# First block's q and k turned by the tensor engine instead of by transposing DMAs, in a kernel of attention and two MLP stages with a written-out sequence

## The chip, the cores and the metric

One core of one Trainium2 chip runs the whole program. The metric is the device time of one execution in microseconds. Before the change, three runs gave 931.09 us as their median (930.62 to 933.18).

## The reference, cut to what matters

```
attention: q, k, v are (4 batches, 8 heads, 576 positions, 64), s is (4, 8, 576)
  scores = q k^T / 8, causal, plus min(-(cum_i - cum_j), 0) with cum = cumsum(max(s, 0))
  out    = softmax(scores) v                      -> x, 2304 rows of 512
first MLP:  h = x w_in (512 to 2048);  x = (h - tanh(h)) w_out
second MLP: a = x w_a, b = x w_b (512 to 1536);  out = (a * b) w_out
```

Heads and batches of attention are independent; each row of x passes through both MLPs by itself.

## The kernel before, in words

Numbers are carried as a high and a low 16-bit part, so that a product of two 32-bit matrices becomes three matmuls of 16-bit parts. Splitting into parts is elementwise work for VectorE (DVE), ScalarE (ACT) and GpSimd (POOL), and there is much of it: q, k, v, the attention weights, x, the hidden values, and all MLP weights, which come as words of 64 bits.

Queries are taken in blocks. Block 0 is batch 0, positions 0 to 255, and its four head pairs are four *units*. For a unit, `qk_split` (L1086) makes the split tile `qk` of 8 slices of 128 columns (four of q, then four of k; in each slice the high and the low part beside each other). `u_turn` (L1107) turns these slices, so that the head dimension lies on partitions: one transposing DMA on SP's queue (`turn`, L1102) writes all 8 slices into `qkT`. Two copies then put half of the partitions (64 of 128) of `qkT` into `qB` and `kB`. These tiles hold three further partitions, the bias rows, which `u_split` (a scaled constant) and `u_load` (a DMA) fill. `u_qk` multiplies `qkT` and then `qB`/`kB` into one sum, `u_exp` and `u_norm` make the split weights `a`. In block 0 the weights are already turned by PE: `u_norm` multiplies each slice with the unit matrix `eyeh` into a `qk` bank and copies it out into `aT`. `u_pv` multiplies with v.

Block 0 goes through the first MLP with unsplit 32-bit matmuls (`l1_mm`, L1315, and `l2_mm`, L1350), because the weights are not yet split; later blocks use split weights.

Operations are recorded in program order, with the engines that may do each (`either`, L356; `copy_scaled`, L930, allows ACT, DVE, and POOL unless its source is PSUM). The string `ORDER` (L38) then fixes both the order of issue and the engine of each: `follow` (L445) reads three characters as one number, whose last two bits choose the engine and whose other bits name the operation. Each engine works through its own operations in that order; semaphores hold one back until its inputs and buffers are ready. Nearly all instructions carry the line of the helper that calls the engine, L647, so the profile is read by tile names. In those names, `qk` is the split tile, the PSUM banks of the scores and the banks of the turned tiles, `ws` and `raw` hold loaded q, k and v, `w` the MLP weights, `zs` the exponentials, `xf` the attention output. POOL instructions that read, and DVE instructions that read two SBUF tiles or copy from SBUF to SBUF fast, are marked by `shares` (L659), and a marked POOL instruction is made to wait for the marked DVE instruction ahead of it in the order.

Of the kernel before, what the change touches and what calls it, by code (L numbers as in the profile page):

```python
# [41 lines left out]
    "AFNAFgAMYAQIAGUAGgAQMAGkAKJAGoAHgAHkAG9APcAPkAYUAh0AHoAPsAGuAPgAH8AP0AGwAHAAHuAG0AZIAHEAh8AKBAHwAG5AHIAKQAKUAKYAKcAKgAH0"
    "AKkAJmAIAALQAFkAMuAM1AKoAQgALcAIEAP4AIIAYYAiQAKsAKyAM6AM8ALBAH5ALEAP8ALIAXwAK0ALgANIAJpALUALYALkANAARAANEAQwARQAlcAYcANM"
    "ANQALMAX0AX4AX8ALoAYgALsALyAK4AYAAK8AMBANUAYEAZQAL0AMEAIMANYANeAIRANtAN8AL4AL9AYIANwAOAAMIAiMAOIANhAUQAPoANkAYOAMMAiIAN0"
    "AYkAOEAjIAiUAOMAOQANpAiYAicAUYAikAigAOUAQkAN4AioAixAOYAMQAOeAOtAisAYoATwAOwAO0Ai9AOgAOkAQoAMVAlqAT4AO5AOoAO8AliAjAAQsAjV"
# [2002 lines left out]
```

## Time and profile before

| what | value |
|---|---|
| median of three runs | 931.09 us |
| the profiled execution | 930.71 us, of which the span of the core is 928.9 us |
| PE busy | 881.3 us (95% of the span), 7650 matmuls |
| DVE busy | 805.7 us (87%) |
| ACT busy | 574.1 us (62%) |
| POOL busy | 346.1 us (37%) |
| DMA queue on SP | 55.6% of 16 engines' span |

The span is counted from the first to the last instruction. Shares over the whole span hide the stages: attention of block 0, then the first MLP between the attention of the following blocks, then the second MLP. So the stretches have to be read one by one. PE is TensorE's matmul row; its ends are modelled.

### The profile page before, as it was taken

To read this page: it belongs to the slowest core of one execution; us is meant where nothing else is said; L and a number is where in the kernel's file an instruction comes from. 1 tells how busy PE (TensorE), PEld (TensorE's weight loads), DVE (VectorE), ACT (ScalarE), POOL (GpSimd) and SP (SyncE) were. 2 spreads that over 40 slices of the span, in tenths; PEclk is the share of its full clock that TensorE was granted. 3 is DMA by queue.
4 is the path that set the end of the run, shared out by engine and by line. 5 is a ranking of instruction groups with operands and counts; after the bars stand their busy time and mean duration, and the time that the engine had idled before them with its cause. 6 is when DMAs were issued, how large, how long until landed. Compare 5 with 4: busy or idle time off the path is not lost.

```text
span 928.9 us, 20616 instructions
## 1 busy us (share of the span) xinstructions
PE 881.3 (95%) x7650; PEld 647.6 (70%) x7650; DVE 805.7 (87%) x2011; ACT 574.1 (62%) x1136; POOL 346.1 (37%) x495
## 2 busy tenths in 40 slices
...
GB/s 204 304 214 238 231 123 124 113 154 171 206 165 174 193 179 167 208 137 161 308 206 189 84 24 1 69 2 1 47 54 53 60 185 65 62 72 112 72 68 115
DMA packets 260197, 123.38 MB, mean 133 GB/s; under 512 B 228544, under 2 KB 236976, under 8 KB 260096
## 3 DMA queue, kind: packets, MB, share of 16 engines
q1 hardware_dynamic: 259936, 121.79, 55.6%
q8 instruction: 60, 0.98, 0.4%
q14 instruction: 41, 0.34, 0.1%
q10 hardware_dynamic: 160, 0.26, 0.1%
...
## 4 chain that ended last, share of the span: by engine, by line
PE 47%; DVE 5%; issue 2%; DMA 1%; POOL 1%; ACT 0%; SPq 0%; POOLq 0%; DVEq 0%; ACTq 0%
PE h L647 16%; PE qk L647 12%; PE acc L647 11%; PE pv L647 8%; DVE w L647 1%; DVE x2f L647 1%; DVE g L647 1%; DMA x2f<-pb_d 0%; DMA out_dram<-x2f 0%; DVE a L647 0%; DVE ghl L647 0%; DVE sq L647 0%; DVE xf L647 0%; DVE h L647 0%; DVE th L647 0%
## 5 line engine op out<-in xcount | busy, mean ns | idle before, releaser
L647 PEld LDWEIGHTS <-w 128*128 128x128 f16 x3840 | 372.2, 98 | 67.0 <-issue 4.0
L647 PE MATMUL h<-xhl,w 128*128 128x256 f16 x2256 | 276.9, 273 | 2.4 <-DVE ghl L647 1.1
L647 PE MATMUL acc<-w,ghl 128*128 128x512 f16 (+1 forms) x1092 | 233.6, 358 | 0.9 <-DVE sq L647 0.9
L647 PEld LDWEIGHTS <-ghl 128*128 128x128 f16 x1290 | 123.6, 98 | 99.9 <-issue 4.8
L647 PE MATMUL h<-xf,w 128*128 128x256 f16 (+1 forms) x416 | 71.3, 310 | 0.0
L647 DVE CUSTOM_DVE_ANT_0 qk<-qk,caus,cs 128x384 f32<-128x384 f32 (+3 forms) x120 | 64.9, 555 | 2.8 <-PE qk L647 1.4
L647 PE MATMUL qk<-xf,w 128*128 128x256 f16 x432 | 55.2, 273 | 0.8 <-DVE xf L647 0.6
L647 PE MATMUL pv<-xf,w 128*128 128x256 f16 x432 | 55.0, 273 | 0.0
L647 ACT ACTIVATE g<-h 128x512 f32<-128x512 f32 x40 | 23.4, 592 | 48.8 <-PE h L647 27.0
L647 ACT ACTIVATE w<-w 128x1024 f32<-128x1024 f32 (+1 forms) x45 | 50.9, 1156 | 1.4 <-DVE w L647 1.4
L647 ACT ACTIVATE th<-h,xc 128x512 f32<-128x512 f32 x64 | 43.7, 683 | 9.5 <-PE h L647 7.4
L647 PE MATMUL qk<-qkT 128*128 128x128 f16 (+4 forms) x168 | 45.7, 316 | 3.7 <-ACT zs L647 3.1
L647 PE MATMUL qk<-kB,qB 67*128 67x128 f16 (+4 forms) x168 | 45.3, 313 | 3.9 <-ACT zs L647 2.2
L647 PEld LDWEIGHTS <-v 128*64 128x64 f16 x1440 | 37.7, 113 | 12.8 <-issue 10.8
L647 PEld LDWEIGHTS <-x2f 128*128 128x128 f16 x360 | 35.1, 98 | 7.1 <-DMA x2f<-pb_d 0.8
L647 DVE SCALAR_TENSOR_TENSOR h<-h,xc,th 128x512 f32<-128x512 f32 x48 | 36.0, 751 | 1.6 <-ACT th L647 1.6
L647 ACT ACTIVATE zs<-qk,nm 128x128 f32<-128x128 f32 (+1 forms) x64 | 30.2, 472 | 11.2 <-DVE nm L647 9.4
L647 DVE SCALAR_TENSOR_TENSOR ghl<-h,xsg,ghl 128x512 f16<-128x512 f32 x48 | 35.8, 746 | 1.4 <-ACT ghl L647 0.9
L647 DVE SCALAR_TENSOR_TENSOR a<-qk,sm,a 128x512 f16<-128x512 f32 (+1 forms) x56 | 35.2, 630 | 1.4 <-ACT a L647 1.0
L647 ACT ACTIVATE qk<-qk,nm 128x512 f32<-128x512 f32 (+1 forms) x56 | 31.7, 566 | 7.4 <-DVE nm L647 5.4
L647 ACT ACTIVATE sq<-qk 128x512 f32<-128x512 f32 x22 | 13.1, 594 | 37.4 <-PE qk L647 35.0
L647 PE MATMUL pv<-aT,v 128*64 128x128 f16 x960 | 34.5, 225 | 1.3 <-DVE aT L647 0.8
...
## 6 DMA issues: line engine op xcount, KB each, us to landing
...
```

The costliest lines, as they stand in the source:

```text
L647: return getattr(getattr(plan.nc, name), what)(*[real(a) for a in args], **{k: real(a) for k, a in kw.items()})
```

## The change

In `u_turn` the units of block 0 (`u.j == 0`) no longer issue the transposing DMA. Each unit instead fills two PSUM banks, one with its four q slices and one with its four k slices, by matmuls with `eyeh`; each bank is copied whole into `qkT` and, by a second copy of 64 partitions, into `qB` or `kB`. A copy that reads PSUM may go to ACT or DVE, not to POOL. All other units keep the old code.

`ORDER` is replaced as a whole. The number of recorded operations goes from 4569 to 4581 (three more in each of four units).

```diff
 ORDER = (
-    "AAMAAEAB0AAIAAQAAUAAAAAYABsAB4ABoABwAAcAAgAAkAAsAAwAA0ABEABJABNABSAAoAA4AA8ABAABVABZABkACEACAAB8ACIACMACQACYAQQAIkACUACc"
...
 )
@@
         qkT = anew(u, [P, n + u.sk, P], F16, "qkT")
-        turn(qkT, u.qk.rearrange("p a e d -> p (a e d)"))
-        copy_scaled(u.kB[0:D], qkT[0:D, n:], 1.0)
-        copy_scaled(u.qB[0:D], qkT[D:P, 0:n], 1.0)
+        if u.j == 0:
+            for which in range(2):
+                pt = bank("qk", 3)
+                pl.hold = (qkT, u.qB if which == 0 else u.kB)
+                a0, m = (0, n) if which == 0 else (n, u.sk)
+                with pl.group():
+                    for i in range(m):
+                        pl.tensor.matmul(
+                            pt[:, i * P:(i + 1) * P], u.qk[:, a0 + i].rearrange("p e d -> p (e d)"), eyeh,
+                            start=(i == 0), stop=True, skip_group_check=True)
+                pt = pt[:, 0:m * P].rearrange("p (a c) -> p a c", c=P)
+                copy_scaled(qkT[:, a0:a0 + m], pt, 1.0, True)
+                if which == 0:
+                    copy_scaled(u.qB[0:D], pt[D:P], 1.0, True)
+                else:
+                    copy_scaled(u.kB[0:D], pt[0:D], 1.0, True)
+        else:
+            turn(qkT, u.qk.rearrange("p a e d -> p (a e d)"))
+            copy_scaled(u.kB[0:D], qkT[0:D, n:], 1.0)
+            copy_scaled(u.qB[0:D], qkT[D:P, 0:n], 1.0)
```

## Rows read from the trace of the kernel before

**Rows 1.** Busy time by stretch: PE, PEld, DVE, ACT, POOL (instructions), granted clock, DMA share, GB/s
```profile
9.40:39.60 30.20, 14.69 (x109) 9.20 (x110) 29.38 (x115) 28.56 (x72) 12.54 (x24) 1.00 1.00 243
39.60:113.00 73.40, 66.88 (x355) 42.52 (x355) 71.13 (x218) 69.96 (x134) 22.93 (x40) 0.98 0.94 241
113.00:440.00 327.00, 324.27 (x3302) 217.39 (x3300) 295.75 (x869) 263.16 (x558) 158.19 (x241) 1.00 0.85 162
440.00:476.00 36.00, 32.17 (x223) 21.06 (x222) 34.65 (x81) 35.32 (x51) 8.47 (x8) 1.00 0.73 257
476.00:900.00 424.00, 422.56 (x3505) 341.53 (x3504) 353.46 (x684) 172.16 (x314) 134.54 (x164) 1.00 0.24 74
900.00:929.00 29.00, 20.44 (x164) 15.72 (x162) 15.68 (x28) 1.72 (x3) 6.63 (x8) 0.90 0.30 96
```

**Rows 2.** Timeline of PE: start us, us, instruction, count, idle time before it
```profile
17.38 0.27 PE L647 MATMUL qk<-qkT 128*128 128x128 f16 x1
...
39.57 1.92 PE L647 MATMUL h<-xf,w 128*128 128x256 f32 x4
...
42.54 1.11 PE L647 MATMUL h<-xf,w 128*128 128x256 f32 x4
```

**Rows 3.** Timeline of SP's queue: the transposing DMAs of units 0 and 1
```profile
13.22 2.81 SPq L647 DMA_TRANSPOSE qkT<-qk  x2
```

**Rows 4.** Groups by form, 10 to 50 us: busy us, mean ns, idle before
```profile
L647 ACT ACTIVATE aT<-qk 128x512 f16<-128x512 f32 x6 | 3.5, 591 | 0.3 <-PE qk L647 0.3
L647 DVE TENSOR_SCALAR aT<-qk 128x512 f16<-128x512 f32 x2 | 1.4, 688 | 0.1
L647 ACT ACTIVATE kB<-qkT 64x512 f16<-64x512 f16 x2 | 1.2, 613 | 0.0
L647 DVE TENSOR_SCALAR kB<-qkT 64x512 f16<-64x512 f16 x2 | 0.7, 336 | 0.0
L647 POOL TENSOR_SCALAR qB<-qkT 64x512 f16<-64x512 f16 x3 | 1.8, 616 | 0.7 <-POOL qk L647 0.5
L647 PE MATMUL qk<-eyeh,a 128*128 128x128 f16 x48 | 7.9, 286 | 2.2 <-POOL a L647 1.1 <-DVE aT L647 0.5 <-ACT aT L647 0.3
```

**Rows 5.** The same view, operations that change engine in the new sequence
```profile
L647 DVE SCALAR_TENSOR_TENSOR v<-ws,sc,v 128x512 f16<-128x512 f32 x1 | 0.7, 745 | 0.0
L647 DVE SCALAR_TENSOR_TENSOR a<-zs,sm,a 128x128 f16<-128x128 f32 x6 | 2.1, 346 | 0.1
L647 DVE SCALAR_TENSOR_TENSOR qk<-ws,sc,qk 128x256 f16<-128x256 f32 x6 | 2.9, 490 | 0.0
L647 DVE TENSOR_SCALAR aT<-qk 128x256 f16<-128x256 f32 x5 | 2.1, 417 | 0.5 <-PE qk L647 0.5
L647 ACT ACTIVATE qk<-ws,sc 128x256 f16<-128x256 f32 x7 | 3.3, 494 | 1.7 <-DVE sc L647 1.7
L647 ACT ACTIVATE w<-w 128x1024 int32<-128x1024 uint16 x4 | 4.5, 1117 | 0.0
L647 POOL TENSOR_TENSOR v<-ws,v 128x512 f16<-128x512 f32 x1 | 1.2, 1153 | 0.1
L647 POOL TENSOR_TENSOR a<-zs,a 128x128 f16<-128x128 f32 x2 | 0.9, 429 | 0.2
```

**Rows 6.** Timeline of DVE: the low parts of unit 0
```profile
10.78 0.88 DVE L647 SCALAR_TENSOR_TENSOR qk<-ws,sc,qk 128x256 f16<-128x256 f32 x2
```

**Rows 7.** Timeline of 440 to 460 us, three instructions
```profile
446.25 0.69 DVE L647 TENSOR_SCALAR w<-w 128x1024 int32<-128x1024 int32 x1
...
454.27 0.16 PE L647 MATMUL pv<-wac,ones 128*128 128x1 bf16 x1 [1.02 <-DVE w L647]
...
455.84 1.24 ACT L647 ACTIVATE w<-w,wsc 128x1024 f16<-128x1024 f32 x1
```

**Rows 8.** Timeline of the last microseconds
```profile
917.68 2.75 PE L647 MATMUL acc<-w,x2f 128*128 128x512 f16 x12
...
924.19 0.75 DVE L647 SCALAR_TENSOR_TENSOR x2f<-acc,wac,x2f 128x512 f32<-128x512 f32 x1 [0.20 <-POOL x2f L647]
```

More of the change, by code (lines that the diff above doesn't have):

```diff
@@ L42 @@
[L42 to L45, printed above, removed]
@@ new lines @@
+    "AD4AE4AJIAJQAF0AGVAC5AGdACtAP0ARMAGQAQgAEsAKEAP4AJUAJYAP9AJgAJcAZoAZsAJkAKQAQBAJoAKUAJtAKoAJxAJ1AQEAKIADwAD0AEwAGkAD8ARQ"
+    "Ai0AE0AEAAKsAKwAKMAJ4ANCAKcAKgAE8AKkAiwAFAAEEAEIANEAEOAEdAEgANKAHkAHoAioAEQANMAFEAZwAFIAFOAFRAigAGwAG0AEkAEoAZ0AFcAFgAQI"
+    "AEUAikAHwAHsAFkAGoAG4AZ8AGsAH0AFpAQ1AG8AFUAFZAKaAHAAEZAQkAHGAHJAZ4AH4ANUANYANdAHVAQMAQQAQ4ANgAM8ANkANoAK0AFsAH8AHMAK4AL0"
+    "AK8AIAAIUAQ8AHYAaAAIYAHcAQcALAASAAHRAIGALEAIJARwAMAAFxAj4AIMAIRAL4AZEAHgAZIALIAJ+ALMALQALlALoAQoAIcAIgAjAAL8ANSAN4ALsALW"
@@ new lines @@
+    "ANsAQsARgAYgALYAN8AZMAMEAMIALcAQYAKBANwALhAN0ATQAOAAYkAYoALwAZQAYsAZYAY0AIkAOsAMMAZUAMQAMWAY4AMlAOEAYwAi8AMZAMoAMsAMwAOw"
+    "AOIAIpAOOAORAOdAOgAO4AMcAMhAY+Ai4AVAAO0AOkAO8APAAOUAOZAjEARUAjIAjMAjUAjQAVIAPEAM0AZcAjYAOoAjhAPIAmMAjcAPOARYAPdAUgAPgAjt"
+    "APkAPQAPUAPYAmaAM5AmSAjwAPpAPsAUoAPwARcAkFAUsAaMAj0AmUAaQAkMAkIAmcAj8AaUAmiAaYAUkAUwAU0AVEAmkAkAARkARoAR0AkQAVMAZAAVQAU8"
+    "AR4AQUARsAZiAawAU4AosAjkAVgAVkAVUASQAagAjoAZkAR8ASgAaEAbUAkVAa0Aa4AakAVoAVsAkaAkoAkcAacAa8AbEAVwAbIASFATgASIAmoAlQAowAbY"
@@ new lines @@
+    "AVYAkgAomAbcAksAkwAVcAkkAlUAbgAlYArCAooAo4ASVAmsASYASMAb4AaIAlcAWAAWIASlAk0ArEAScASwAV0AmwAm0Aq6Ak4AWEAb8AaoAWMASoAlEAo2"
+    "AboATUAk8AlgAlkAbsAV4AV8AcAAccAasASsAdAAWgAloAq8AbNAcgAWoAWsAlAAlsAl4Am4AWQAogAbQAo9AnkAbyAWkAckAS0AlIAl8Am8Az8AlwArMAWU"
+    "ApCAdEAdIAcEAbkAnAAlMAcMATYAWwAnEAnwAn0An4AS4Al1AcIATAAWcAcQAb0AnIAnoAnsAmAAcoAdMAnMAcwA0IATkAdUAnQAToAcsAc0ArKA0AA0EAdY"
+    "AcVAS8An8AdkApEA0QAnUAWYAcYAnZA0MATEApIAc6ApMAoAAW0Ac8AoEAoIAoNAdeAmEAncAngAmIATIAp4ArSAdoAdsAoQAoUA0UAW8AdwAbAA58Ad4Ap8"
@@ new lines @@
+    "AqAAd8ATMAqEApQAqIA0YAqMAW4AeIApUArWATcAqQAdgApYAXAAqUApcAXEATsAeMATwA0cAXIAXMAqYAeQArYArcApgAeUA0gAqhA0kAqdAeAA3oAUAAXg"
+    "AXoApsAeEApwAecAqkAoYAodArkAXQAsMApmAegAXUAppAXsAroArgAesAewAe0AXkAemAp0AsQAfQAT0ArsA0oAeoAfUAqoBFYArwA0sAT4A0wAr0Ar6AsU"
+    "AsYAsAAfYAscA00AsgAXwAT8AXcA1UAskAr8AeYA1iAsoAUEAs0BFsA05AsuAX0AXYAe4AsxAsEAqsA08AX4A1YAfcA1IAfAAs4AUIAfEA1cAqwAf0A30A1k"
+    "A1MAUMAX8AYAAYEAYIAYMAfJA34AfMA3sAUQAUVAsIAgYA3wAUYA1QAUcAYQAs8AtAA1sA1qA1yA3+AfkAdQBFgAtEAgcAggAtIA1AAg8AfoAf4A4AA10A4I"
@@ new lines @@
+    "AfgAd0A6IA8UAf8AYUAgkAtMAtQA8cAYcA4EAgoAtUAtcAhgAtgAgAAgsAtlA2sAtYAtoAgIA6AAhkAgEA1FAtxA6NAhAAhEAgwAhIA2EAhMA14A18Ae8AuQ"
+    "A2IAuYA2wA2AAucA2MAuUBFkAhoAgMA20AhsAt1At5AtsA6EAt8BFcA8YA2QA8gAuAAugAhwA4YA6UAfsAuEBF8A2UA2aAuJA4MA4cA4gAu4A4QA2dAu8AhQ"
+    "Ah4AukAuoAfwAvAAYYAusAgSA4UA2gAhUBGAA2kAvEAh0Ah8A4kAgUBF0A6YAvgA4oAvIAvkA5AA5MAiAA40BF4AvMA5QA5EAvoBGEAvQA8QAvsAg2AiEAiU"
+    "AwIAg4AwMAiMAvwAwQAwUA44A2oBFwAiQAiYA4uA4xAv0BGMA5UAhaAvUA5IBGQA5YAuMA5cA24A8oAwYA6dAuwAu0A28AhcAv4AvcA8mAv8AwcA48AvYBGI"
@@ new lines @@
+    "BGUA5oBGYAwwA6SAw4BGcBGkBGgA3AA3EBGoBFoA6gA5gAw8AwgBJoBGtA5sBHMA6sBJgA3IA5lA5wAwkA3MA3VBHRAwAA6wA8sA6kA6oBGwA3YA60Aw0A3R"
+    "A3cBHUBHAA7gA7kA8yBG1A64BHYA7UBHgBJtA7oBJcAxYAxcBG5AxgAwEA7YAxkAiJA68A7JA7MA7cA7sBJkBJ0BHIA80AxAA7AA7wA78A7EA70A9AAxEA3g"
+    "A8AA7QA84BG9A90AxoA88AxJA75A9EAwsAxsA94BHcA9IA3lBHFBOQA98A9oA9sA9wA8EAyAA9MA9QBJ8A9cAyIAyEAyMBOIA+AA+EAxMBOEA50BHqBHlBHs"
+    "BL0AyoA+IBL8A9gA9WA54A+RA9YAyQBIsBHwBH0BOMA9kA+MBIwBI0BOVA+UA+YAwoAxwBIgBIkBH4BH8BIoBIABJwAxUBMAA8IBJ5A8MBI4BL4BIEBIIBI8"
@@ new lines @@
+    "BJCBIVBLwBJIBIMBJEAywBKABKEAx1BMIBJMBKIBIRAxQAyUAyYBKMBIYBOcBKQBKUBKYAysBK0AycBKcBKpA+cBJQA+gA+kBKiBKkAy0BLABLEAy4Ax4BK4"
+    "A+oBK8A+sBMSBKsBMGAx8A+wA+0A/NBLIA/RA+4Ay8A+8A/UBLMBLQBIcAykBMMBMUAzAAzEBKwA/CBLUBLZBMgBMkBLcBLgBOmAygBMoBMYA/EBMcBMsBNU"
+    "BNYBOYBJUBNIBNMA/YBMwAicA/cBOgAzMA/IBNQA/oBNcA/sA/0A/4A/wBNgBLkBNkAzUBM8A/gBNxBN0A/lBM2BNqBJYA/8BNABOoBO0BM5BNtBN4BNEBOs"
+    "BOwBO4BO8BAABPcBPgBAUBAcBPoBPABPEBAEBPKBPNBLoBPkBPQBPsBPwAzIBAIBPUBPYBP0BP4BP9BQEBQABAgBA8BBEAzQBQIAzYBLsAzkBQMAzcBAYAzg"
@@ new lines @@
+    "AzoAzwAz0AzsBBABN8BOBBAQBQQBAkBAoBAuBAwBQUBQYBBkBBsBBIBQcBBoBXYBBwBAMBQgBXgBA4BXcBBMBBQBX0BBUBBYBXwBQkBQoBRABB0BXoBQsBB4"
+    "BXkBA0BXsBCMBQwBCUBBgBBcBB9BCABX8BXMBQ2BQ4BREBRIBXUBRMBYABRQBXQBRcBX4BYEBZQBYIBCQBYMBYUBC0BYQBYYBZEBYcBcEBCYBC8BC4BDAAz4"
+    "BCEBCIBY6BY8BZIBCcBCgBZYBCkBZABZMBCoBDcBDgBCsBYsBcIBYyBY0BDEBCwBe4BYgBYkBDIBZWBZhBQ9Be8BRUBRZBfIBfQBYoBfMBZcBZkBZoBZwBZs"
+    "BZ0BZ4BfUBfABakBaoBDOBDkBDoBfcBDRBfgBaYBZ8BaABfEBEEBEMBEQBfYBEIBDsBasBaGBaMBaJBacBagBDwBDYBD1BaQBfkBawBD4BbUBbMBa0Ba6BbB"
@@ new lines @@
+    "BfoBa9BbEBbQBbYBcMBDUBcWBaUBfsBfwBRgBRkBf0BEUBEYBf4BcQBbcBgABf8BRoBbgBdMBckBRsBgEBgJBgmBgZBEdBbkBg8BbIBcYBgwBEgBboBEABEo"
+    "BdQBbuBcoBgcBdUBRwBbwBb0BgMBg4BD8Bg0BccBgRBgoBcgBggBcsBcwBSIBSQBc0Bc6BtkBdABEwBdYBeIBdcBdgBeMBR0BtoBEkBEsBtsBj0BSUBgtBR5"
+    "BE0BdkBE4BR8BSMBE8BSYBtwBFEBuIBhEBc9BdoBd1BeABgVBeEBt4Bt0BScBb4BSwBdsBb8BS0BS4Bt8BtcBhCBhMBeQBS8BeUBFMBhJBhQBtYBdEBdwBd4"
+    "BTABTYBuABFIBuMBtgBFQBSiBuEBTEBSlBFBBcABhcBeYBecBeiBhUBhYBhgBhkBTgBekBj4BSEBTkBuQBdIBd8BuUBuYBucBugBSABTIBhoBeoBukBuoBvG"
@@ new lines @@
+    "BusBuxBTcBvJBi4BhsBh4BvNBjABhwBFUBu4Bi8BSoBh8BjEBjwBToBiQBiEBvcBvQB1IBTMBSsB1MBiIBvUBvkBUoBTUBjIB1EBesBkABh0BjMBvYBiMBiU"
+    "BjQBiYBj9BTsBkQBvhBkEBicBigBUsBTwBisBikBT0BjUBjYBkIBkMBipBUABiwBu8BUIBkUBjcB1QBkYBUEBvABkcBkgBkmBksBUwBl0BlsB1cBlwBl4BUM"
+    "BUQBu1Bl8BTQBiABk4BU0BvtBkwBmABlEBvqBe0B1wBk8BmEBT8BlABkpBi0BewBUUBlIBvwB1UBlMBU4BjgBmIByUBlQBlUBUZBlaB1oBv8B1kBU8Bv0BT4"
+    "BlgB1YBv4BlkB10B1sBUcB1gBwABjkBV4BWABmOBmRBV8BwEByYBVBBVEBk0BwIBjsBxgBxYBjpBxkBwMBWEB14BwYBldB18BxcB2ABVQBVUBmUB2EB2MB2Q"
@@ new lines @@
+    "BycB2IB2UBxoBxsByQBwQBVYBwcBVcB28B2YB2yB20BxwBx0BygBwwBwkB24BUkBloBx6B3IBwoBwsB2kBw0BVgBUgBx8B3EBw4Bw8B0UBVkCDkB0MCDoB0Y"
+    "BVoBxABxMBmYCDsBxEBmcBwUBykBVsBVMBmkBxQB2dB0QB3BBwgBmgBWIByoCD0CEQCD4CD8BV0B0cBmoBxJBysBVIBVwBWMBWQBmsBmwBm4Bm0BnMB3NBnQ"
+    "B0gBm8BywBzkBnUBWUBzYBnABy0BnJBy4B0kB0oBWYB2qBnYB3QBWgByABnEBy8BzABzcB2gBxUBWcBWkBoUB3UBnsBn0CDwBnwBn4BncBngBocB2sBnoBzN"
+    "BoYBzgBzoB0uBWoB3YBzsB0wB5EBWsBzEBzwBz0CEABn8BWwB0AByEBW4BnlBzQCEEBzJBoACEMBoECEIByIBXBCEUB3cBogB0EBokB5IBz6B6EBoIB3oB5M"
@@ new lines @@
+    "Bo8BpEBXEB3gBpABooBzUBz9B3sB6JB00ByMBpkBW8B0IB5QB6OCEYCEcB5UBpoB58BW0CEgCEkBpIB3kB3wB30B34B6CCEsB5YB5cBosCEoCEwCE0B38B5g"
+    "BowB4BB5mB4EBoQB4QB4UCFQB4cBXIBpMB4gCE5BoMBo0B4kB4IBpQB5oB4YCFcB4oBpUB6QB4sB6UB4wB04B6YB74BpYB78B41BpsCFoCFVB44B48B4MB6c"
+    "B6gCFIBpcCE8B5sCFBB1BB6kB8AB5AB6oB6sBpwB64B8EB8ICFgCFwBqMB8MBqQBp0B8QB8UBqUB08BqYB7QBp4B7UB7YCFlB7EB7IB7MCFZCIkB68Bo4B7c"
+    "BpgCFFB8aB7gBp8BqcB7kB7sBqAB6yCF4CLcB5wB7oB7wB61BqgCLgCFsBq0Bq8B50BqECLYBrACF0B8cBq4CFMB70CF8CGICIcB54CGACIqBqICHsBqlB7A"
@@ new lines @@
+    "B8gCIiCLkCIuBrEBrIBrOCGECGMCLsCHkBrcCHwCHoCGQCGUCLoCH0CGYCH4BqoBrkCG8BroCGwCHACH8BrgCLwBqsCHECLUCG0CG4CGeBrRCGgCHICGkCGo"
+    "CIACI8BrsCIECJACJECHMCHSCMAB8kCHVCHZCHcB8oCIwCI0CI4BrwBqwBr1Br4BsEBsIBsMCLQBsQCIJCL0CKgCL4B8tCL8CMECMIB8wCJICJMBsUCMMCMQ"
+    "CMUBrYCMYCMcCMhCGsCM8CJYCKkCHgB80CJQCJkB84CJwBsAB88CNKB9ABrUB9ECNUCJoCJsB9IBr8CIMCNACNMCJcCNRCNcCJ0CKYBsYCMwCaIB9MCJ4CMk"
+    "CZ8CNECNYCaACIQB9YB9dB9QCJ8BscCJVB9gCM0CaEBsgCKcCNhB9kCKoB94B9oB+ACMpCKACZ4CQMCNkCM4CQQCKsCKwCKMBskBssBsoCZ0BswB+ECIYB98"
@@ new lines @@
+    "CN0B+gCNoB+kCMsB9VCKECaYCIVB9sB9wB+IB+oB+sCKQCagBs0Bs4CK0CKICJgBs8CZwBtEB+MB+RB+wB+UB/wBtICNsCNwCK6CK9CN4B90B/0CaMB+0CaU"
+    "CPYBtMBtBCN8COACPcCOEBtQCOQB/4B/8COUCaQCQWB/ICOoCOsCOKB/QCakCPQCQIB+cCLAB+6CQYCPUB/MCOcCPgB+8CacCaoCOgCOMB+YCKUCOwBtUCas"
+    "CPkCPoCawCPsB/UCOkCPwCb0Ca4Ca8Ca0CO0CbBCO4B/YCP0CLECPECSEB/cCbcCPICboCbFCO+B/gCAACQcCbkCPACSMCSQCbwB/kCQgCLICSIB/AB/ECOY"
+    "CbUCbQCBACbJCbNCBICQkCAECPMCBECAICbhCbtCSUCRQCSYCewCQoCAMCRcCBMCQsCb6CQwCAYCAgCbYCRgCRUCBQCP4CBUCRYCScCSgCb8CQ0CRkCQ4CQ9"
@@ new lines @@
+    "CAcCAkChoCREChwCh4Ce1B/oCAoCRoCiACLMCRsCBoCSkCAsCBwCR5CRyB/sCP8Ce6CR8CcACcGCQACSoCiECh8ChgCR0CRBCcICcMCAwCcQCRICcUCcYCA0"
+    "CccCBsCAQCd4CdwCcgCckCcpCCQCiQCeuCctCB0ChsCd0CcxCd8ChkChcCiICQFCAUCc0CeACh0CB4CA8CRMCiMCiUCB8CBYCiYCA4CicCikCioCSACigCSs"
+    "CCUCBcCeECjUCitCjICdICeICiwCi1CCBCi5CdMCeMCCECeoCjZCdQCeQCc8CdACjMCdECBgCe8C6ACfACSwCfECi9CeUCgkCdUCgsCdYCjRCdlCjdCdeCCY"
+    "CCcCS0CjgCgoCS5CS8CTACfICdoCTECTICTQCTUCCgCTMCTlCTpCgwCThCjACjoCc4CeYCBkCCkCCMCCICCoC6ECfMCTtCdgCfwCTwCdsCfQCg0Cf8CTYCjy"
@@ new lines @@
+    "Cg4CCsCCwCjECf0CTcCf4CfUCC0CfYCjtCg8ChACmYCjmCC4CmcCgACfkCT0CT4CT8CC8CDACDECgECfoCUECUICDMCfcCj0CgICDICfgChECecCekCgMCDZ"
+    "CegCgYCj4ChJCj8CDcCUMCUQCkACUsCU0CfsClkCgcCgSCgVCUUCUYCUwCDQClcCU4CUcCkECUgCDUCmiChMCV8CWEC6ICmmCloCggCkIClgCkMCkQCU8Cls"
+    "ClwC6MCUoCk0CmUCl0CkoCl4CkUCUkC6QCksCVACkcCk4Ck8CkgCl+CmBCkYChQCVFCkwCkkClAClECmEClRClUClICoQCVUCVcCVYCoUChUCVgChYCVJC6U"
+    "CUAC6YC6cClNCWICVkCoYCocCogCVoCncCokCVMCm0CmoCooCngCWACnkCosCm4CmsCVQCVsCm8CVwCnoCWMCmwCoyCV0CWQCnACWUCWYCnECnICnRC6kCns"
@@ new lines @@
+    "CnwClYCnUCo1CmICnNCmQCXMCXUCXYCXQCn0CWkCWoCn4Cn8CoBCWsCWwCo4CmMCoFCnYCoICXcCoMCV4CWgCWcC6gCXgCW0CW4CXmCXoCW8CXACX0C6oCo8"
+    "CpFCpACDgCX8CYcCYkCv8CwACwECYACwICwMC6uC6wCwlCwpCwQCwUCX4CYoCpICpMCpQCwtCpUCpYCpcCpgCpsCwwCYECYICpxCpkCp1Cp5Cp8CqAC3kCYg"
+    "CYsC3oC2wCqECXEC4YCpoCXIC60CXsCYMC3sC20CXwCqJCw0Cw4CYwC+ECYQCqQCqYC24CwaCwcC3wC30CqUCYYCY1CYUC28C3ACqcC4dC4gCY4C3EC3ICwg"
+    "CqgCY8C3MC5MC34CZAC65Cq4C4kC38C3UC68Cq8C4oC4sC4AC7ACrAC3YC+IC4wC4IC3eCqkC7EC3gC7oC40C4MCrEC48CrICqoCZICrMCZEC7IC4SC5AC5E"
```

157 lines of the change are left out of this document (47 added, 110 removed).

## The prediction, written before the result was known

> **What bounds the kernel now.** I read the share of busy time first (PE 95%, DVE 87%) and then cut the span into stretches, because PE is idle for only 47.6 of 928.9 us and the question is where. The busy times by stretch [rows 1] answer it. Before 9.4 us there is nothing to do but load. From 9.4 to 39.6 us, the attention of block 0, PE is busy for 14.7 of 30.2 us, DVE for 29.4 and ACT for 28.6: the elementwise engines set the pace and PE follows. From 39.6 us, where the first 32-bit product of the first MLP starts [rows 2], to 113 us PE is 91% busy and DVE and ACT 97% and 95%. From 113 to 440 us PE is busy for 324.3 of 327 us, from 476 to 900 us for 422.6 of 424: there PE is the bound and what was late stays late. Two places are left: 440 to 476 us, where the second MLP's weights are split, ACT is 98% busy and PE idles for 3.8 us; and the last 8.6 us after PE's last product [rows 8]. A change at the start therefore counts by what it does to the moment at which PE becomes the bound.
>
> **The change part by part.** *What goes from the path.* The two transposing DMAs of units 0 and 1 are issued from 13.22 us and hold SP's queue for 2.81 us [rows 3]; the first score product runs at 17.38 us [rows 2]. The low parts of unit 0 end at 10.78 + 0.88 = 11.66 us [rows 6], so PE could turn unit 0 from there: eight matmuls of at most 0.29 us each [rows 4] and two rounds of copies at 0.6 to 0.7 us put the first score product near 14 us, some 3 us earlier. The freed SP time lets weights and later blocks start loading earlier; in this stretch no engine's row waits long for a load, so I count it at nothing.
>
> The Trainium skill (VectorE: DVE Perf Modes, "The three transpose paths") gives 390 ns for a 128x128 transpose by TensorE and 1309 ns by the DMA crossbar. Per slice the trace is kinder to the DMA: 17.38 - 13.22 = 4.16 us for sixteen slices, 0.26 us each, copies included. By the page's figures unit 0 alone would have saved 8 x 0.92 = 7.4 us; I keep the trace's 3 us, and only for a rival below.
>
> *What comes instead, unit by unit.* The matmuls are 4 x 8 = 32, at most 0.29 us each, 9 us at most and nearer half, since they overlap; PE is idle for 15.5 us of that stretch [rows 1], so they cost nothing unless PE's order makes a later product wait behind them. The copies cost more. Before there were eight of 64 partitions from SBUF: reading the old order string, two on ACT at 0.61, three on DVE at 0.27 to 0.34, three on POOL at 0.62 [rows 4]. Now there are sixteen that read PSUM; in the new string eleven are on ACT and five on DVE. Their price is that of the copies into `aT`, which do the same thing: 0.59 on ACT, 0.69 on DVE [rows 4] (both had 128 partitions; a copy of 64 partitions takes no less, as the 0.61 shows). So ACT gains 11 x 0.59 - 2 x 0.61 = +5.3 us, DVE 5 x 0.69 - 3 x 0.32 = +2.5 us, POOL -1.9 us.
>
> *What the new sequence moves to make room.* I decoded both strings (operation and engine, three characters each) and compared what lies ahead of the first 32-bit product. DVE loses to POOL the low part of v (0.75), three low parts of weights (3 x 0.35), and a few setup and preset operations (about 1.2 in all), and to ACT one scaling (0.45); it gets two low parts of q and k from POOL (2 x 0.49), a shift of weight words from ACT (0.69, [rows 7]), and two copies into `aT` and one scaling from ACT (3 x 0.42 to 0.49) [rows 5]. That is -3.4 + 3.0 = -0.4 us. ACT loses v's scaling (about 0.6, a 512-column operation), three scalings of q and k (3 x 0.49), the shift (1.12), the two copies and two scalings (about 1.7), and gets back two scalings (0.95): -4.0 us. POOL, whose subtraction takes 1.15 us for v and 0.43 for weights [rows 5], ends with about 4 us more, between 2 and 5. **Sum for the stretch to 39.6 us: DVE +2.1, ACT +1.3, POOL +4 us.** Counted the same way to the last product of block 0 in the first MLP (about 113 us) the surplus is still there: both sequences hold nearly the same operations ahead of the same PE step, so nothing is put off.
>
> *What of it ends late.* DVE has 30.2 - 29.4 = 0.8 us of idle time in the stretch to take some of the 2.1 us; ACT has 1.6 us for its 1.3. So the first 32-bit product comes between 1.3 and 2.1 us later if DVE's sum decides. From below, the earlier scores could save up to 3 us if waiting, not work, ended the stretch; from above, POOL's 4 us could fall on DVE. I take +1.7 us, because DVE's row is the fullest. One small credit: the first 32-bit products ran at 1.92 us for four, later ones at 1.11 [rows 2]; if PE is kept busier before, up to 0.8 us of that goes. I count none of it.
>
> *The rest.* To 440 us PE is full, and the order of its steps is locally permuted with the same steps; I count zero, with at most the 2.7 us of idle time there to gain. In 440 to 476 us the new string gives ACT two operations that DVE had (a 128x1024 split at 1.24 us [rows 7] and a 512-column scaling, about 0.7) and DVE others of equal length: between 0 and +1.2 us (1.9 less ACT's 0.7 us of idle time [rows 1]), and I take zero, since DVE's rows ended most waits there, such as the 1.02 us one [rows 7]. In the last microseconds the final four product groups, the last ten DVE operations and the stores have the same order; zero.
>
> **Sum.** The profiled execution took 930.7 us (span 928.9 and 1.8 around it); +1.7 gives 932.4. The median of the runs is 0.4 above the profiled one, so I predict 932.8 us. With this kernel 0.3% (2.8 us) is about what can be told from no change, so "same" reaches from 928.3 to 933.9.
>
> **The rivals.** *A: the early scores win.* If the start-up is a chain of waits rather than a sum of work, all that follows moves forward by the 3 us: 928.1. For it: PE is idle for half of the stretch [rows 1], and the first score product waits for a transposed tile. Against it: DVE is 97% busy from 9.4 us on, so an earlier tile only changes which work it does first.
>
> *B: POOL's work falls on DVE (slower).* The kernel marks POOL instructions that read, and DVE's two-input and fast SBUF ones, as sharing a port and makes POOL take its turn. If DVE is held while POOL runs, the 4 us more on POOL come on top of the 2.1 of DVE: 931.1 + 1.7 + 4 = 936.8. It decides from the point at which POOL's instructions lie beside DVE's two-input ones instead of beside its PSUM reads. For it: more of POOL's new work is low parts, up to 1.15 us in one instruction. Against it: POOL is busy for 12.5 of 30.2 us and DVE is idle for only 0.8, so today it costs little. The Trainium skill (SBUF — State Buffer, "SBUF: two separate sides") calls the shared port pair an exclusive lock for the whole instruction, against a VectorE operation with two SBUF inputs too; by it the full 4 us could appear as longer or later DVE instructions, which is this rival's price.
>
> *C: the delay is taken up before 113 us.* PE idles for 6.5 us between 39.6 and 113 us; if a part of that does not hang on DVE, a later start disappears there: 931.1. Against it: DVE and ACT are full in that stretch as well.
>
> *D: ACT ends the weight split.* The 1.2 us at 440 to 476 us are added to the forecast: 934.0.
>
> *E: the new sequence removes waits in mid-run.* Half of PE's 7.9 us of idle time between 113 and 900 us away, against the start's 1.7: about 928.5 to 929, and with A as well about 926.
>
> **How the numbers follow.** Forecast 40% (931.3 to 934.0), A 17%, B 13%, C 12%, D 10%, E 8%. Faster by over 0.3% are A and E in their better halves and both together: 23%. Slower by over 0.3% are B, most of D, and the forecast's upper edge: 29%. The rest, 48%, is the same within 0.3%. The range for 8 in 10 leaves out the far ends of A with E, and of B: 926.8 to 937.2.
>
> **What would show it.** Right: the first score product near 14 us, no transposing DMA before those of the next block, sixteen copies at 0.6 to 0.7 us, the first 32-bit product at 41 to 42 us, PE's stretch after 113 us unchanged and 1 to 2 us late. Wrong by A: that product at 37 us or before, with DVE less than 95% busy ahead of it. Wrong by B: DVE instructions longer than 0.5 us where they took 0.49, or DVE idle time behind POOL of some microseconds. Wrong by D or E: the idle time of PE in 113 to 440 or 440 to 476 us changes by more than 1 us.

## The result, and the profile after

The changed kernel is slower: 936.29 us (median of five runs, 935.28 to 938.71) against 932.94 us for the kernel before beside it (930.62 to 934.61). The ratio is 1.0061, 95% interval 1.0044 to 1.0077. That is some 5.7 us, where 1.7 were forecast; the time itself lies 3.5 us above the 932.8 of the forecast, within its range. The two medians as they stand differ by less, 3.4 us. The ratio is followed here, because the profiled executions and a second set of runs (e5 below) stand on its side: the profiled one took 936.72 us, its span 934.9 us, 6.0 us more than before. Two single runs far above all others are left out of every figure: one of e6 (958.40 us, at a mean clock of 0.946) and one of the kernel before beside e8 to e10 (2365.12 us).

Busy time by stretch, as in [rows 1] (PE, PEld, DVE, ACT, POOL, granted clock, DMA share, GB/s), with one row more that ends at the first 32-bit product:
```profile
9.40:39.60 30.20, 15.83 (x111) 10.62 (x112) 27.56 (x95) 27.41 (x64) 13.58 (x27) 1.00 0.91 259
39.60:113.00 73.40, 68.42 (x360) 44.26 (x360) 69.51 (x212) 68.96 (x135) 23.15 (x41) 0.98 0.82 211
113.00:440.00 327.00, 319.61 (x3274) 214.58 (x3273) 291.31 (x866) 265.03 (x563) 159.67 (x241) 1.00 0.85 159
440.00:476.00 36.00, 34.05 (x234) 22.92 (x232) 32.91 (x77) 33.75 (x48) 9.19 (x14) 0.95 0.72 263
476.00:900.00 424.00, 422.29 (x3489) 340.01 (x3487) 356.43 (x705) 173.88 (x312) 132.54 (x160) 1.00 0.24 75
9.40:42.90 33.50, 18.52 (x140) 12.71 (x141) 30.86 (x115) 30.68 (x74) 16.18 (x31) 1.00 0.91 263
```
DVE's column is the one to read. Before, DVE was idle for 0.8 us between 9.4 us and the first 32-bit product; now it is idle for 33.50 - 30.86 = 2.6 us. The row from 113 to 440 us matters too: PE is idle there for 7.4 us, where it was idle for 2.7 (some 2 us of the difference lie before 120 us, where block 0's stage now ends later).

The timeline of PE, as in [rows 2], with the first score product and the first two 32-bit products:
```profile
15.27 0.26 PE L647 MATMUL qk<-qkT 128*128 128x128 f16 x1 [2.24 <-DVE qB L647]
...
42.91 2.02 PE L647 MATMUL h<-xf,w 128*128 128x256 f32 x4
45.44 1.76 PE L647 MATMUL h<-xf,w 128*128 128x256 f32 x4
```
The scores start 2.1 us earlier than before, and the first 32-bit product runs 3.3 us later (42.91 against 39.57).

The copies by form, 10 to 50 us, which answer to [rows 4]:
```profile
L647 PE MATMUL qk<-eyeh,qk 128*128 128x128 f16 x32 | 4.4, 306 | 4.3 <-DVE qk L647 3.0 <-DVE aT L647 1.0 <-ACT kB L647 0.3
L647 ACT ACTIVATE qkT<-qk 128x512 f16<-128x512 f32 x7 | 4.0, 578 | 0.5 <-PE qk L647 0.4
L647 DVE TENSOR_SCALAR qB<-qk 64x512 f16<-64x512 f32 x3 | 2.0, 691 | 1.3 <-ACT qkT L647 1.2
L647 ACT ACTIVATE kB<-qk 64x512 f16<-64x512 f32 x3 | 1.7, 573 | 0.0
L647 DVE TENSOR_SCALAR qkT<-qk 128x512 f16<-128x512 f32 x1 | 0.7, 692 | 0.0
L647 DVE TENSOR_SCALAR kB<-qk 64x512 f16<-64x512 f32 x1 | 0.7, 672 | 0.0
```
The prices are the forecast ones. The third row carries what was not forecast: 1.2 us of DVE's idle time ahead of a copy into `qB`, ended by ACT's copy into `qkT`. The timeline of all engines, 13 to 17 us, shows the place:
```profile
13.92 0.57 ACT L647 ACTIVATE qkT<-qk 128x512 f16<-128x512 f32 x1
...
14.52 1.30 DVE L647 TENSOR_SCALAR qB<-qk 64x512 f16<-64x512 f32 x2 [1.25 <-ACT qkT L647]
```
No data goes from one copy to the other. Both read the bank of unit 0's turned q; ACT reads it at 13.92 us, and DVE's copy starts when ACT's has ended. (Of the two copies merged into this line, the first is unit 0's.)

The third thing to see is the granted clock. Windows of the changed kernel, then of its second profile (e5), then of the kernel before (columns as above; 0.50 is 1.2 GHz, 1.00 is 2.4 GHz):
```profile
84.00:88.00 4.00, 1.83 (x22) 1.29 (x22) 4.00 (x10) 4.00 (x9) 1.33 (x2) 0.97 1.36 231
88.00:91.00 3.00, 3.00 (x8) 1.17 (x7) 2.79 (x11) 2.59 (x7) 1.77 (x3) 0.50 1.25 198
459.00:463.00 4.00, 2.13 (x19) 1.64 (x17) 3.83 (x9) 4.00 (x10) 1.76 (x2) 1.00 0.19 33
463.00:467.00 4.00, 4.00 (x24) 2.95 (x23) 4.00 (x12) 4.00 (x6) 0.00 (x0) 0.57 1.04 376
```
```profile
112.00:116.50 4.50, 2.09 (x24) 1.31 (x24) 3.83 (x19) 3.31 (x7) 1.98 (x3) 1.00 0.84 188
116.80:120.20 3.40, 3.40 (x14) 1.80 (x13) 3.09 (x14) 3.23 (x8) 1.26 (x4) 0.51 0.33 74
```
```profile
80.00:83.40 3.40, 3.26 (x21) 1.36 (x20) 3.40 (x10) 3.40 (x7) 1.12 (x1) 0.51 1.30 235
459.00:463.00 4.00, 3.12 (x22) 1.95 (x20) 3.97 (x10) 4.00 (x7) 1.86 (x2) 1.00 1.03 381
```
While PE has work, the kernel before has one fall to the lower level, from 80.0 us. The changed kernel has two, from 87.7 and from 463.2 us (in e5 from 86.1 and 116.8 us), each 3.4 us long. Ahead of the second, PE was busy for 2.13 of 4 us. At half clock PE does 1.7 us less in 3.4 us, so the 1.9 us by which PE is busier in 440 to 476 us (34.05 against 32.17) are about what it then loses.

In this profile, however, the second fall is not what makes the loss larger than the late start, because the excess is there before it. The eight small products into `pv` from `xmx`, which are spread over the first MLP, mark the way; the kernel before, then the changed one (first and last start, us):
```profile
L647 PE MATMUL pv<-xmx,ones x8: 163/167/172, 111.5 to 436.1; 128*128 128x1 bf16 x8
L647 PE MATMUL pv<-xmx,ones x8: 163/165/167, 116.1 to 443.3; 128*128 128x1 bf16 x8
```
The changed kernel is 3.3 us late at the first 32-bit product, 4.6 us at the first of these, 7.2 us at the last, and 6.0 us at the end of the span. The second fall comes at 463.2 us, behind the last of them. The second profile (e5), without a fall there, goes from 7.7 us late at the last (443.8 us) to 6.2 at the end, so by this comparison that fall costs some 0.3 us.

### The profile page after: what moved, and what is told of

Its sections match the earlier page's. It is cut to its first block, busy times and chain, and to the rows that moved or that the text cites. A ratio compares the mean times of both kernels' runs of the same rounds, so it can differ in the third digit from the quotient of the medians.

```text
span 934.9 us, 20654 instructions
## 1 busy us (share of the span) xinstructions
PE 887.1 (95%) x7682; PEld 653.9 (70%) x7682; DVE 803.2 (86%) x2012; ACT 576.9 (62%) x1135; POOL 351.2 (38%) x507
## 4 chain that ended last, share of the span: by engine, by line
PE 70%; DVE 15%; ACT 5%; issue 4%; DMA 4%; SPq 1%; POOL 0%; POOLq 0%; DVEq 0%; ACTq 0%
PE h L647 25%; PE acc L647 19%; PE qk L647 15%; PE pv L647 10%; DVE w L647 2%; DVE a L647 2%; DVE qk L647 2%; SPq L647 1%; DVE ghl L647 1%; ACT sq L647 1%; DMA w<-in_moe_w_a_dram 1%; DVE h L647 1%; DMA w<-in_moe_w_out_dram 1%; DVE g L647 1%; DMA aT<-a 1%
## 5 line engine op out<-in xcount | busy, mean ns | idle before, releaser
L647 ACT ACTIVATE sq<-pv 128x512 f32<-128x512 f32 x22 | 13.1, 594 | 40.3 <-PE pv L647 37.7
L647 ACT ACTIVATE zs<-qk,nm 128x128 f32<-128x128 f32 (+1 forms) x64 | 30.2, 472 | 11.5 <-DVE nm L647 9.0
```

What stands on the lines that cost most here:

```text
L647: return getattr(getattr(plan.nc, name), what)(*[real(a) for a in args], **{k: real(a) for k, a in kw.items()})
```

## The experiments

Theory 1: the loss is the late start, made by the copies out of PSUM, and is carried to the end. Its rivals: the late start grows by itself on the way (theory 2); the new sequence loses in mid-run (theory 3); the start is a chain of round trips and not a sum of work. Losses below are (ratio - 1) times 931 us, the median of the kernel before beside these runs; their 95% intervals are 1.2 to 2.0 us either way.

| run | first 32-bit product, us (later than before) | ratio, 95% interval | loss, us | mean granted clock of the runs |
|---|---|---|---|---|
| e1 new start, old rest | 43.01 (+3.4) | 1.0037 (1.0022 to 1.0052) | 3.4 | 0.9959 |
| e2 old start, new rest | 39.31 (-0.3) | 0.9998 (0.9985 to 1.0011) | -0.2 | 0.9958 |
| e3 qB of unit 0 on ACT | 42.46 (+2.9) | 1.0048 (1.0029 to 1.0067) | 4.5 | 0.9943 |
| e4 edit in old sequence | 52.59 (+13.0) | 1.0141 (1.0123 to 1.0160) | 13.1 | 0.9948 |
| e5 changed kernel again | 43.02 (+3.4) | 1.0066 (1.0053 to 1.0080) | 6.1 | 0.9928 |
| e6 copies from SBUF | 46.11 (+6.5) | 1.0098 (1.0077 to 1.0119) | 9.1 | 0.9938 |
| e7 copies twice | 46.69 (+7.1) | 1.0088 (1.0070 to 1.0106) | 8.2 | 0.9950 |
| e8 units 2, 3 by DMA | 42.62 (+3.1) | 1.0031 (1.0012 to 1.0050) | 2.9 | 0.9962 |
| e9 unit 0 alone by PE | 45.01 (+5.4) | 1.0059 (1.0039 to 1.0079) | 5.5 | 0.9949 |
| e10 the same, old rest | 44.90 (+5.3) | 1.0057 (1.0039 to 1.0076) | 5.3 | 0.9954 |
| e11 unit 1's copies on ACT | 43.99 (+4.4) | 1.0051 (1.0032 to 1.0070) | 4.7 | 0.9952 |
| e12 v's low part on DVE too | 43.24 (+3.7) | 1.0040 (1.0026 to 1.0053) | 3.7 | 0.9947 |

The products are those of one profile each. The kernel before has a mean clock of 0.9949 to 0.9960 beside them. The first five runs of the changed kernel had 0.9948, where e5 has 0.9928. The mean also counts a fall behind PE's last product, which every profile here has and which PE does not feel: the granted clock from 900 us to the end is 0.90 before [rows 1] and 0.94 after the change, which is 0.0031 and 0.0022 of the mean.

**e1 and e2: which part of the sequence.** Both are cut at the first 32-bit product.
```diff
 e1: PE's turns, new sequence up to the first h<-xf,w
-    new sequence from there
+    sequence of before from there
 e2: DMA turns, sequence of before up to the first h<-xf,w
-    sequence of before from there
+    new sequence from there
```


> The changed kernel's operations, in the changed sequence up to the first 32-bit product and in the old sequence from there on. In the two profiles the changed kernel is 3.3 us late at that product, 4.5 us at the end of block 0's stage, 6.6 us near 440 us and 6.0 us at the end. Theory 1 (the late start is carried and the rest of the new sequence adds its own share): the first 32-bit product near 42.9 us, the total 3.0 to 4.0 us above the kernel before. Theory 2 (a start 3.3 us late meets other loads and splits and grows by itself): the total 5 to 6.5 us above. Theory 3 (the start is caught up and all of the loss is in the rest): within 1 us of the kernel before.

> The other half: the old transposing DMAs and copies and the old sequence up to the first 32-bit product, the new sequence from there on. Theory 1: first 32-bit product near 39.6 us as before, total 2 to 3 us above the kernel before. Theory 2: within 1 us of the kernel before. Theory 3: 5 to 6 us above.

The start alone loses 3.4 us, as much as its first 32-bit product is late. The new rest alone loses nothing that can be told. Theory 3 falls. Of theory 1, the second half falls too: the rest has no share of its own. Of theory 2, e1 is against it (5 to 6.5 us) and e2 fits it.

**e5: the whole change again.**


> The changed kernel once more, beside the kernel before and the other kernels of this call. Its start with the old rest cost 3.5 us and its rest with the old start nothing, so theory 1 (the loss is the start's, carried to the end) expects 3 to 4.5 us above the kernel before; theory 2 (start and rest together lose more than each alone) 5 to 6.5 us.

The loss is 6.1 us, so theory 2 gave the better number: start and rest together lose 2.7 us more than the start alone (the intervals, 4.9 to 7.4 and 2.0 to 4.8 us, just part). The clock is a rival that is not shown. For it: the mean is 0.9928 against 0.9959 in e1, a difference of 0.0031, and one fall of 3.4 us is 0.5 x 3.4 / 930 = 0.0018 of the mean and at most 1.7 us. Against it: the first five runs had 0.9948, hardly less than e1, and lost 5.7 us; in the first profile the excess stands before the second fall; and the profiles of e9 and e11 have a second fall as well (from 117.7 and 462.9 us), with losses that are no larger than their late starts. What the traces do show is idle time of PE: from 113 to 440 us it is 7.4 us here in the first profile, 6.2 in e5, 5.2 in e1 and 4.1 in e2, against 2.7 before. The largest part behind a late start are waits for ACT's sums of squares (`sq`): 3.0, 2.5, 1.6 and 0.6 us.

**e4: was the new sequence needed?** The sixteen copies stand on the engines of the new sequence, at the places of the old DMAs and copies, moved only where the buffers asked for it.
```diff
 sequence of before
-SP turn; kB<-qkT; qB<-qkT                        (each of four units)
+PE 4 x qk<-eyeh,qk; qkT<-qk; kB<-qk; the same for q
```


> The edit alone: PE's turns and the sixteen copies on the engines that the new sequence gives them, but put at the places of the old DMAs and copies in the old sequence, all else as before. Theory 1 (the copies' work and their waits are what makes the start late, whatever the sequence): first 32-bit product at 42 to 44 us, total 3 to 5 us above the kernel before. Rival (the new sequence's own choices make it late, the edit does not): first 32-bit product at 39.5 to 41 us, total within 1.5 us of the kernel before.

It loses 13.1 us, about three times what theory 1 gave. DVE's timeline shows why, with three long waits for ACT:
```profile
18.91 0.69 DVE L647 TENSOR_SCALAR qB<-qk 64x512 f16<-64x512 f32 x1 [1.76 <-ACT qkT L647]
...
33.98 1.22 DVE L647 SCALAR_TENSOR_TENSOR w<-w 128x1024 int32<-128x1024 int32 x1 [3.98 <-ACT w L647]
...
44.87 0.69 DVE L647 TENSOR_SCALAR qB<-qk 64x512 f16<-64x512 f32 x1 [3.94 <-ACT qkT L647]
```
The first and the last are, as in the changed kernel, for a copy out of the bank that DVE is to read, which on ACT stands behind other work; ahead of the middle one ACT itself had waited 2.90 us, at 31.76 us, for a turn by PE. So the new sequence does not add the late start to the edit. It takes back 9.6 of the 13.0 us that the edit costs in the old one, as placed here; another placement might cost less.

**e3: the wait for the other reader of the bank.**
```diff
-DVE  qB<-qk   (unit 0, at 14.52 us)
+ACT  qB<-qk   (unit 0, right behind qkT<-qk of the same bank)
```


> The changed kernel with one instruction moved: unit 0's copy into qB, which on DVE waits until ACT has read the same PSUM bank (idle 1.25 us at 14.52), goes to ACT right behind ACT's copy of that bank. DVE has 0.69 us less to do and 1.25 us less to wait, ACT 0.59 us more. Theory 1 (DVE's waits on the other reader of a bank are a part of the late start): DVE's idle time at 14.5 us gone, the first 32-bit product 1 to 1.9 us earlier, at 41.0 to 41.9 us, and the total 1 to 1.9 us below the changed kernel. Rival (the start is a sum of work over ACT and DVE, or another chain takes over): the product moves by less than 0.5 us either way, the total too.

The wait of 1.25 us is gone, but the product comes only 0.46 us earlier: the rival's number. The total, 4.5 us above the kernel before, is 1.2 to 1.6 us below the changed kernel's 5.7 and 6.1, which theory 1 had; the intervals cannot tell it from either. DVE's timeline, which now has two waits in its place:
```profile
15.63 0.40 DVE L647 TENSOR_SCALAR ws<-cum,sig 32x256 f32<-32x256 f32 x1 [0.72 <-POOL v L647]
16.36 1.23 DVE L647 SCALAR_TENSOR_TENSOR w<-w 128x1024 int32<-128x1024 int32 x1 [0.34 <-ACT w L647]
```
POOL's v is the low part that the new sequence took from DVE [rows 5]; it frees the buffer that DVE fills next.

**e6 and e7: less and more copying.**
```diff
 e6
-copy_scaled(u.qB[0:D], pt[D:P], 1.0, True)
+copy_scaled(u.qB[0:D], qkT[D:P, 0:n], 1.0)      # kB likewise; 5 of 8 on POOL, 3 on DVE
 e7
+for again in range(2):
     copy_scaled(u.qB[0:D], pt[D:P], 1.0, True)   # kB likewise
```


> The changed kernel, but the eight copies beneath the bias rows read the turned tile in SBUF, as before the change, so that POOL can do five of them (0.62 us each) and DVE three at 0.3 us; for unit 1 the two copies out of PSUM stand on DVE where its copies beneath the bias rows stood. ACT has 5 copies of 0.57 to 0.59 us less, DVE some 1.1 us less, POOL 3.1 us more; the chain of one unit gets longer by a copy behind a copy. Theory 1 (the start ends when the work of ACT and DVE is done, and the copies out of PSUM are 3.7 us more of it on the two): first 32-bit product 1.5 to 2.2 us earlier than in the changed kernel, at 40.7 to 41.4 us, total 1.5 to 2 us below it. Rival (the start is a chain of round trips between PE and the copies): first 32-bit product at 42.9 us or later, total not lower.

> The changed kernel with each of the eight copies beneath the bias rows done twice, the second right behind the first on the same engine: 4 more of 0.58 us on ACT and 4 more of 0.69 us on DVE, 5.1 us over the two. Theory 1 (sum of the work of ACT and DVE): first 32-bit product 2 to 3 us later than in the changed kernel, at 45 to 46 us, total 2 to 3 us above it. Rival (chain of round trips, in which these copies are hidden for the most part): less than 1.2 us later.

e6 went the other way: 3.2 us later, although ACT and DVE had less to do up to the product (2.5 and 0.9 us). Theory 1 as a sum of the work of both falls. POOL's copies stood ahead of its v, and DVE waited for that, by DVE's timeline:
```profile
18.87 0.40 DVE L647 TENSOR_SCALAR ws<-cum,sig 32x256 f32<-32x256 f32 x1 [2.84 <-POOL v L647]
```
It is no clean test of the copies from SBUF. e7 is 3.8 us later at the product, more than theory 1's 2 to 3, and more than the 2.75 us that DVE alone was given. It also shows the bank's order the other way round, on ACT's timeline:
```profile
18.08 0.60 ACT L647 ACTIVATE qkT<-qk 128x512 f16<-128x512 f32 x1 [0.60 <-DVE qB L647]
```

**e8: is it ACT?**
```diff
-if u.j == 0:
+if u.j == 0 and u.p < 2:                          # units 2 and 3 by DMA, as before
```


> The changed kernel with units 2 and 3 turned by DMA again (units 0 and 1 by PE), their copies beneath the bias rows from SBUF on DVE (0.28 to 0.40 us) and POOL (0.62 us). In the changed kernel these two units were turned 7 to 8 us before their first score product, so their round trips are not late. ACT loses 7 copies, 4.0 us; DVE loses 0.69 and gets 0.68; POOL gets 1.24. Theory 1 (sum of the work of ACT and DVE): first 32-bit product 1.5 to 2 us earlier than in the changed kernel, at 41 to 41.4 us. Theory 1b (DVE's path alone ends the start; ACT's copies are hidden): first 32-bit product less than 0.7 us earlier. Total below the changed kernel by the same, or by 1.7 us more where PE is not left at half clock a second time in the run (3.4 us each time).

Busy time from 9.4 to 42.9 us, columns as above:
```profile
9.40:42.90 33.50, 16.67 (x125) 11.16 (x126) 30.65 (x116) 27.59 (x68) 18.27 (x33) 1.00 0.98 281
```
ACT has 3.1 us less to do (27.59 against 30.68), DVE the same, and the product is 0.3 us earlier. This is the number of theory 1b: ACT's copies of these two units are hidden. Whether DVE's path ends the start, as 1b has it, was left to e9 and e11. With no fall of the clock in its profile while PE has work, and the highest mean clock of the table, e8 loses 2.9 us.

**e9 to e12: emptying DVE's path.** e9 and e10 take unit 1 to the DMA as well; e11 and e12 start from e8.
```diff
 e9, e10
+if u.j == 0 and u.p < 1:                          # e10: sequence of before from h<-xf,w on
 e11
-DVE  kB<-qk; qB<-qk; qkT<-qk   (unit 1)
+ACT  the same three
 e12, beside e11
-POOL ws<-ws,sc; v<-ws,v        (v's low part)
+DVE  v<-ws,sc,v                (ahead of unit 0's qB<-qk)
```


> As the run before, and unit 1 by DMA too: its two copies of 0.67 and 0.69 us beneath the bias rows and its 0.69 us copy of k leave DVE (2.05 us), ACT changes 0.57 for 0.61 us, POOL gets 0.62. On DVE these three stand between 14.5 and 16.6 us; what is behind them can start from 15.4 us, when POOL ends v's low part, whose buffer it takes. Theory 1 and 1b: first 32-bit product a further 1.2 to 2 us earlier, at 39.5 to 40.5 us (theory 1) or 40.5 to 41.5 us (1b). Rival (a chain of waits that goes round these copies): no earlier than in the run before.

> The start of the run before, the old sequence from the first 32-bit product on. If the rest of the new sequence is neutral, the same total as the run before within 0.7 us; if the new rest loses more where it starts late (3.5 us of loss with the old rest, 5.9 with the new), less by about the same share.

e9 did not answer its question. DVE's timeline, then that of SP's queue, have the reason:
```profile
32.85 0.28 DVE L647 TENSOR_SCALAR kB<-qkT 64x512 f16<-64x512 f16 x1 [2.68 <-DMA qkT<-qk]
```
```profile
21.27 5.53 SPq L647 DMA_TRANSPOSE qkT<-qk  x1
```
Unit 2's transposing DMA held the queue for 5.53 us, and DVE waited for it. e10 has the same start and the same loss (5.3 against 5.5 us), so behind this late start, too, the new rest is neutral.

> The run with units 2 and 3 by DMA showed ACT's copies of these units to be hidden: 3.1 us less of ACT's time moved the first 32-bit product by 0.3 us. Now the time so won on ACT takes unit 1's three copies from DVE (0.67, 0.69 and 0.69 us, where they stand at 11.9 and from 15.1 to 16.6 us); all else as in that run. Theory 1b (DVE's path ends the start): first 32-bit product 1 to 2 us earlier than there (42.62), at 40.6 to 41.6 us; DVE would wait for POOL's v until 15.4 us, which keeps some 0.8 of the 2.05 us. Rival (the loads' sums of squares on ACT, PE's sum and DVE's norms between 15 and 20 us are a chain of their own): less than 0.5 us earlier.

> As the run before, and v's low part, which the new sequence had moved from DVE (0.74 us in one instruction) to POOL (0.69 + 1.16 us, done at 15.4 us), back on DVE ahead of the copy into qB, where DVE waits in any case. Then no work of DVE waits for POOL's v. Theory 1b with POOL's share in it (what POOL was given comes back to DVE as a wait): DVE's instruction on the next load's buffer starts at 14.5 us or before where it stood at 15.4 to 16.6, first 32-bit product up to 0.8 us earlier than in the run before. If POOL's v is not on the path: no change, or up to 0.7 us later by DVE's added work.

e11 takes 2.05 us of work from DVE and is 1.4 us later than e8, where theory 1b had it 1 to 2 us earlier. So it is not shown that DVE's path by itself ends the start. Its DVE timeline:
```profile
15.42 0.40 DVE L647 TENSOR_SCALAR ws<-cum,sig 32x256 f32<-32x256 f32 x1 [0.18 <-POOL v L647]
21.36 0.49 DVE L647 SCALAR_TENSOR_TENSOR qk<-ws,sc,qk 128x256 f16<-128x256 f32 x1 [0.70 <-ACT qk L647]
...
31.83 0.28 DVE L647 TENSOR_SCALAR kB<-qkT 64x512 f16<-64x512 f16 x1 [1.04 <-DMA qkT<-qk]
```
At 15.42 us DVE is 1.2 us ahead of the changed kernel (16.58). It gives 0.7 us back where ACT, with the copies put ahead of a scaling, is late, and 1.0 us to unit 2's DMA. e12 has the same two waits (0.70 and 0.62 us); its product is 0.75 us earlier than in e11, about as theory 1b had it for v's low part, though only 0.4 us of it was won by 15 us.

## Why the prediction was wrong

**The sign was right, and so was the carrying of a late start to the end; the size was not.** The edit does what it says: no transposing DMA for block 0, sixteen copies at 0.57 to 0.69 us, 32 matmuls of 4.4 us in all, which PE hides. The first score product came at 15.27 us where "near 14" was forecast, since ACT does two other operations before it copies unit 0's q, and DVE's copy into `qB` comes behind ACT's. Early scores were worth nothing (rival A), and nothing was made up by the end (rival C): in e1, e2, e4 and e8 to e12 the loss is the lateness of the first 32-bit product, within 0.4 us, which is closer than the intervals could promise.

**The work was sized well, the loss in two parts was not.** Of the 5.7 us, 3.3 are the late start, where 1.7 were forecast, and some 2.4 come after the first 32-bit product, where nothing was. From 9.4 us to that product DVE has 1.5 us more (30.86 against 29.38), ACT 2.1, POOL 3.6; the forecast had 2.1, 1.3 and 4.

**The step that failed first is "DVE has 30.2 - 29.4 = 0.8 us of idle time in the stretch to take some of the 2.1 us".** The idle time was not used up. It grew by 1.8 us, to 2.6, so the product came 1.5 + 1.8 = 3.3 us late and not 1.7. A sum of DVE's work was the wrong measure. In the changed kernel, e3, e4, e6, e8, e9, e11 and e12 DVE has 29.7 to 31.3 us of work from 9.4 us to that product, whatever was moved, against 29.4 before; what differs is its idle time, 2.6 us here, 2.5 in e3, 2.8 in e8, 3.5 in e12, 4.6 in e11, 5.9 in e9, 6.7 in e6 and 11.9 in e4, in nearly the order in which the product comes later. (e7 adds work as well: 33.6 us, with 3.7 idle.) I had priced the copies by their durations alone and asked what they delay, but not what they wait for. The largest wait, 1.25 us, is that for the other reader of a bank; the next are 0.39 us for ACT and 0.34 and 0.24 us for PE. The Trainium skill (PSUM — Partial Sum Buffer, "PSUM bank collisions raise a hardware error") has the rule: accesses of two engines to one bank and the same group of 32 partitions must not overlap, reads against reads included, and software has to put them in order. The traces agree as far as they go: one copy waited for the other in both directions (1.25 us on DVE here, 0.60 us on ACT in e7), and no run lets the two overlap. The page would have foretold that a pair of copies of one bank, split over ACT and DVE, does not run side by side.

**Taking one wait away does not give its length back.** e3, e11 and e12 each remove a wait or some work from DVE's path and find the next wait close behind: POOL's v, ACT's scaling, a DMA. In the start DVE and ACT are both full, and each waits for the other. So the 1.25 us are the largest single wait, but not shown to be the cause of the late start: in e3 they were worth 0.46 us. The row on which the forecast rests (DVE 97% busy) says only that the old sequence fits its own operations; a sequence with eight copies more does not inherit that.

**Rival B** had the wrong mechanism and a grain of truth. DVE's instructions are no longer than before (474 ns against 490 for the low parts [rows 5]), so POOL does not stretch them. But v's low part on POOL frees its buffer at 15.4 us, which is what DVE waits for as soon as it is quicker (0.72 us in e3, 2.84 us in e6).

**The second step that failed is the zero for the rest.** It holds for the new sequence behind the old start (e2) and, behind e9's start, for new against old rest (e10); rival D's longer weight split did not come, since PE is idle for less in 440 to 476 us (1.9 us, not 3.8), which is E's sign there. But in the whole change 2.4 to 2.7 us are lost after the first 32-bit product, and the prediction's own sign for the rest was passed: PE's idle time from 113 to 440 us rose from 2.7 to 7.4 us, the opposite of E. The forecast also had no term for a second fall to 1.2 GHz in mid-run. There is one in both profiles of the changed kernel, at 463.2 us in the first, after the excess, and at 116.8 us in the second. Where the mean clock is lowest, in e5, e6 and e3, the loss exceeds the lateness by most (2.7, 2.6 and 1.6 us); but it does by 1.1 us in e7 with a clock of 0.9950, and not at all in e12, e4 and e9 (0.9947 to 0.9949).

Two figures of the prediction are off by themselves, and the forecast does not use them: E with A gives 931.1 - 3 - 4.0 = 924.1 us and not about 926, and PE's last product ends 8.5 us before the end [rows 8], not 8.6.

**What stays open.** Why this kernel loses 2.4 to 2.7 us more than its late start, while e1, with the same start, and e2, with the same rest, do not. The second fall of the clock can be a part of it in e5, at most 1.7 us; in the first profile the excess is PE's idle time before that fall. No run was made in which the kernels differ in the clock alone. It also stays open which waits make the start late, and how much of it could be won back: no version tried starts the 32-bit products before 42.46 us with a turn by PE.
